# Idle matmuls on zeros in four-wide pieces: 19 of up to 512 columns in place of 73 of 128

## The chip, the core and the metric

The kernel runs on one core of one Trainium2 chip. The metric is the device time of one execution in microseconds; where several executions are given, it is their median. Profiles are of one execution, and their clock starts with the first instruction of the span.

## What is computed

Four batches of eight attention heads (768 tokens, 64 columns to a head) feed a two-layer network. Heads 0, 2 and 6 attend to all earlier tokens; the others attend to the last 64 tokens and to the first four.

```python
scores = scale * q @ k.T                       # each batch and head
keep = causal & (retrieval_head | is_sink | in_window)
a = softmax(where(keep, scores, -1e9))
x = (a @ v).transpose(0, 2, 1, 3).reshape(3072, 512)
h = x @ w_in                                   # 512 -> 2048
g = maximum(h, 0) + alpha * minimum(h, 0)
out = g @ w_out                                # 2048 -> 512
```

## The kernel before

The heads are worked in 16 segments of two heads (four segments to a batch). Of a segment, q, k and v are loaded by SP (`L`), cast to bf16 by VectorE, ScalarE or GpSimd (`C`), transposed (`T`; in the first half of the segments on TensorE, with copies `t` out of PSUM, later by DMA), multiplied to scores (`S`, lines 414, 424 and 431), masked (on TensorE at lines 463 and 502 in batch 0, on VectorE after it), exponentiated by ScalarE (`s`), multiplied with v (`A`, line 553), divided by the row sums (`a`), and transposed into `xT` (`X`). The network runs over eight blocks of tokens: `P` is the first layer (line 598), `p` and `g` its leaky ReLU on ScalarE and VectorE (lines 603 and 610), `O` the second layer (line 618), and `o` the copy out and the store. The very last 128 rows of the output go in three column pieces (`L0` to `L2`, lines 637 and 646).

One list, `ORDER`, written out by hand, says in which order the items are issued; each engine works its own instructions in that order. An engine that comes to an instruction whose data are not there waits, and all behind it on that engine waits too. PSUM has eight banks that the code hands out itself: `take` gives the bank that has been free the longest, `give` returns it.

The change touches the items `warm0` to `warm8`. Each is a run of matmuls on TensorE of a tile of zeros, `busy` (128 x 128, bf16, filled by a VectorE memset at the start), with itself, into a bank that nobody reads before it is written anew. The numbers of matmuls are set here (line 725):

```python
for i, n in enumerate((32, 3, 14, 4, 4, 4, 4, 4, 4)):
    item(f"warm{i}", warm, n)
```

Where they stand on TensorE, by `ORDER`: `warm4`, `warm0` and `warm5` (4 + 32 + 4 = 40 matmuls) are TensorE's first work, ahead of the transposes of the first q and k (`Tq0.0`, `Tk0.0`, line 362). `warm2` (14) follows those transposes, ahead of the first scores (`S0.0.0`, line 414), which need the copies `tq0.0` (ScalarE, line 369) and `tk0.0` (VectorE, line 387). `warm3` and `warm6` (8) stand ahead of twelve transposes (line 364). `warm7` (4) and `warm8` (4) each stand ahead of scores of batch 0 (line 414). `warm1` (3) is TensorE's last work, behind `L1`.

Of the kernel before, what the change touches and what calls it, by code (L numbers as in the profile page):

```python
# [74 lines left out]
def kernel(  # L75
# [13 lines left out]
    nc = tc.nc  # L89
# [54 lines left out]
    def take(*choices):  # L144
        got = min((c for c in choices if all(age[b] >= 0 for b in c)), key=lambda c: max(age[b] for b in c))
        for b in got:
            age[b] = -1
        return got

    def give(got):  # L150
        for b in got:
            age[b] = stamp[0]
            stamp[0] += 1
# [3 lines left out]
    def bank(b):  # L157
        return P[:, b, :]
# [91 lines left out]
    busy = const.tile([128, 128], bf16, name="busy")  # L250
# [432 lines left out]
        nc.vector.memset(eSv[:, i, 5, 192:SLOT].bitcast(fp32), 0.0)  # L683

    def warm(n):
        held["w"] = got = take(*ANY)
        for i in range(n):
            nc.tensor.matmul(bank(got[0])[:, 0:128], busy, busy, start=True, stop=True)  # L688
        give(got)

    def load_w_in(n):
# [33 lines left out]
    for i, n in enumerate((32, 3, 14, 4, 4, 4, 4, 4, 4)):  # L725
        item(f"warm{i}", warm, n)
# [60 lines left out]
    for t in range(8):  # L787
        w = TOK[t][1]
# [59 lines left out]
```

## Time and profile before

| | |
|---|---|
| time, three executions | 228.04, 228.27, 229.32 us; median 228.27 us |
| time of the profiled execution | 228.43 us |
| its span | 225.8 us |
| TensorE matmuls | 221.6 us busy (98%), 2005 instructions |
| TensorE weight loads | 136.5 us (60%), 2005 instructions |
| VectorE, ScalarE, GpSimd | 149.1, 140.1, 45.9 us busy |
| the 73 idle matmuls (line 688) | 7.1 us with TensorE in them |

The 2.6 us between the profiled execution's time and its span lie outside of what the profile shows. PE is the matmul side of TensorE, PEld the loading of its stationary operand, which runs beside the matmuls. A matmul's duration in the profile runs from its start to its modelled end, and the matmuls of a stream overlap; so what a matmul costs in a stream is the distance between two starts, and the duration of a row of x n matmuls is n - 1 such distances and one duration. A row of the timeline reads: start, duration, engine, line, operation, output and input, shapes, how many; in brackets the idle time of the engine ahead of it and what ended that.

### The profile page before, as it was taken

What the parts mean: (1) busy time and instruction counts of PE and PEld (TensorE: products, weight loads), DVE (VectorE), ACT (ScalarE), POOL (GpSimd) and SP (SyncE); (2) the same over time, 40 slices, a digit from 0 to 9 for tenths busy, and PEclk for the clock granted to TensorE, in tenths of its full rate; (3) what the DMA queues carried; (4) which work ended last, traced back from release to release, by engine and by line L of the source; (5) the groups of instructions that cost most, each with busy time, mean ns of one, the idle gap of its engine ahead of it and who ended that gap; (6) DMA issues with size and microseconds to landing.
All of it is one profiled execution on the core that took longest, in us unless ns stands there. A gap on an engine that the chain in (4) does not pass through costs nothing.

```text
span 225.8 us, 5241 instructions
## 1 busy us (share of the span) xinstructions
PE 221.6 (98%) x2005; PEld 136.5 (60%) x2005; DVE 149.1 (66%) x393; ACT 140.1 (62%) x286; POOL 45.9 (20%) x91
## 2 busy tenths in 40 slices
PE   7999999999999999999999999999999999999994
PEld 7989876575556557564556455456556555664454
DVE  5798648986659618897899029977486536866000
ACT  3788669999898036587992147786584237563311
POOL 5679749600230001000400001000110100000000
PEclk9999999999999999999999999999999999999999
DMA  6999999999999999999989999976924420000213
GB/s 201 311 240 214 281 223 285 197 196 231 204 284 182 117 232 231 170 167 190 268 160 177 226 243 129 238 156 117 119 94 38 120 93 0 0 3 1 93 68 119
DMA packets 95417, 37.39 MB, mean 166 GB/s; under 512 B 82440, under 2 KB 93600, under 8 KB 95392
## 3 DMA queue, kind: packets, MB, share of 16 engines
q1 hardware_dynamic: 89136, 27.73, 65.2%
q0 software_dynamic: 5792, 8.93, 17.5%
q10 hardware_dynamic: 464, 0.40, 0.6%
q8 instruction: 15, 0.25, 0.5%
q14 instruction: 10, 0.08, 0.1%
HBM read 27.71 MB, written 6.29 MB: 151 GB/s over the span
## 4 chain that ended last, share of the span: by engine, by line
PE 98%; DVE 0%; issue 0%; DVEq 0%
PE P L598 37%; PE P L618 36%; PE P L553 7%; PE P L431 4%; PE P L414 3%; PE P L688 3%; PE P L364 2%; PE P L637 2%; PE P L424 1%; PE P L502 1%; PE P L578 1%; PE P L463 0%; PE P L362 0%; DVE kT L387 0%; DVE ot L646 0%
## 5 line engine op out<-in xcount | busy, mean ns | idle before, releaser
L610 DVE SCALAR_TENSOR_TENSOR g<-neg,oma,P 128x256 bf16<-128x256 f32 (+1 forms) x128 | 70.9, 608 | 36.9 <-ACT neg L603 36.4
L598 PE MATMUL P<-xT,w_in_b 128*128 128x512 bf16 (+1 forms) x512 | 86.6, 326 | 0.0
L618 PE MATMUL P<-w_out_b,g 128*128 128x512 bf16 x368 | 85.3, 379 | 0.0
L603 ACT ACTIVATE neg<-P 128x512 f32<-128x512 f32 x96 | 54.2, 600 | 26.3 <-PE P L598 20.9
L598 PEld LDWEIGHTS <-w_in_b 128*128 128x128 bf16 x512 | 49.5, 98 | 32.3 <-DVE g L610 0.2
L618 PEld LDWEIGHTS <-g 128*128 128x128 bf16 x368 | 33.9, 98 | 37.2 <-issue 1.0
L470 ACT ACTIVATE eR<-P 128x448 bf16<-128x448 f32 (+4 forms) x63 | 36.9, 635 | 5.8 <-PE P L431 2.5
L624 ACT COPY ot<-P 128x512 f32<-128x512 f32 x23 | 13.9, 605 | 37.1 <-PE P L618 32.3
L628 POOL DMA_DIRECT2D out_dram<-ot x18 | 10.3, 572 | 111.0 <-ACT ot L624 110.8
L518 ACT ACTIVATE eS<-P 128x352 bf16<-128x352 f32 x45 | 20.8, 489 | 3.4 <-PE P L431 3.0
L564 DVE TENSOR_TENSOR xn<-P,rcp 128x448 bf16<-128x448 f32 (+1 forms) x32 | 19.5, 608 | 1.1
L529 DVE TENSOR_TENSOR eS<-eS,ms_near 128x352 bf16<-128x352 bf16 x45 | 14.9, 346 | 0.6 <-ACT eS L518 0.5
L563 DVE RECIPROCAL rcp<-P 128x7 f32<-128x7 f32 (+1 forms) x32 | 6.3, 198 | 10.9 <-PE P L553 10.8
L480 DVE TENSOR_TENSOR eR<-eR,mr_near 128x128 bf16<-128x128 bf16 (+5 forms) x54 | 10.7, 227 | 4.3 <-ACT eR L470 4.1
L414 PE MATMUL P<-qT,kT 128*128 128x192 bf16 (+14 forms) x68 | 11.2, 251 | 0.2 <-DVE kT L387 0.2
L553 PEld LDWEIGHTS <-eS 128*128 128x128 bf16 x260 | 9.5, 97 | 2.3 <-issue 0.6
L553 PE MATMUL P<-vb,eS 128*128 128x65 bf16 x260 | 10.7, 193 | 0.0
L431 PE MATMUL P<-qT,kT 64*128 64x176 bf16 (+10 forms) x168 | 10.5, 252 | 0.0
L431 PEld LDWEIGHTS <-kT 64*128 64x128 bf16 x168 | 6.7, 94 | 6.2 <-issue 5.5
L553 PE MATMUL P<-vb,eR 128*128 128x65 bf16 x276 | 10.5, 193 | 0.0
L553 PEld LDWEIGHTS <-eR 128*128 128x128 bf16 x276 | 9.5, 97 | 1.3
L646 DVE COPY ot<-P 128x128 f32<-128x128 f32 x1 | 0.3, 291 | 14.3 <-PE P L637 14.3
(95 smaller groups left out, 177.3 us busy)
## 6 DMA issues: line engine op xcount, KB each, us to landing
out_dram<-ot POOLq DMA_DIRECT2D x18, 256.0 KB, 3.9
kf<-in_k_dram SPq DMA_DIRECT2D x21, 192.0 KB
qf<-in_q_dram SPq DMA_DIRECT2D x18, 192.0 KB
vf<-in_v_dram SPq DMA_DIRECT2D x14, 196.0 KB
qf<-in_q_dram SPq DMA_DIRECT2D x7, 384.0 KB
vf<-in_v_dram SPq DMA_DIRECT2D x12, 192.0 KB
w_in_b<-in_moe_w_in_dram POOLq DMA_DIRECT2D x8, 256.0 KB, 9.6
w_out_b<-in_moe_w_out_dram POOLq DMA_DIRECT2D x4, 512.0 KB, 13.9
```

The source lines that it names most:

```text
L414: nc.tensor.matmul(to, keys, queries, start=True, stop=stop)
L431: nc.tensor.matmul(to, keys[own], queries[own], start=True, stop=True)
L470: nc.scalar.activation(ebuf[n, hh][:, lo:hi].rearrange("p (x c) -> p x c", x=len(parts)), P[:, got[0]:got[0] + len(parts), 0:(hi - lo) // ...
L518: nc.scalar.activation(slots, sc[:, 0:352].rearrange("p (s c) -> p s c", c=176), AF.Exp, scale=scale)
L529: nc.vector.tensor_tensor(slots, slots, ms_near[:, 0:2, :] if m == 0 else ms_near[:, 1:3, :], op=ALU.mult)
L553: nc.tensor.matmul(pav[:, i, :], e[:, o:o + 128], vv[:, j, hh, 0:D + 1], start=(m == 0), stop=(m == len(terms) - 1))
L564: nc.vector.tensor_tensor(xn[n][:, 0:nt, D * hh:D * hh + D], pav[:, :, 0:D], rcp.to_broadcast([128, nt, D]), op=ALU.mult)
L598: nc.tensor.matmul(psg[:, w * i:w * (i + 1)], w_in_b[:, c, 128 * fb:128 * (fb + 1)], xT[:, c, o:o + w], start=(x == 0), stop=(x == 3))
L603: nc.scalar.activation(neg[t, f], bank(held["P", t, f][0]), AF.Relu, scale=-1.0)
L610: nc.vector.scalar_tensor_tensor(g_buf[t % 2][:, fb, 0:w], neg[t, f][:, c], oma[:, fb:fb + 1], bank(got[0])[:, c], op0=ALU.mult, op1=ALU.add)
L618: nc.tensor.matmul(bank(held["O", t, s][0]), g_buf[t % 2][:, f, 128 * s:128 * (s + 1)], w_out_b[:, f, :], start=(f == 0), stop=(f == 15))
L624: nc.scalar.copy(ot, bank(got[0]))
```

## The change

`warm(n)` issues its matmuls in pieces of up to four. The stationary operand is still `busy`. The moving operand is `busy` read w times in a row, through an access pattern with a step of zero, and the output is 128 * w columns of the bank. So 32, 14, 4 and 3 matmuls of 128 columns become 8 of 512; 3 of 512 and one of 256; one of 512; and one of 384: 19 in place of 73, with 9344 columns in both. A weight load goes with each matmul, so there are 19 in place of 73 of these too. All else, `ORDER` included, is as it was: the order and the waits of all other instructions are the same on every engine.

```diff
     def warm(n):
+
         held["w"] = got = take(*ANY)
-        for i in range(n):
-            nc.tensor.matmul(bank(got[0])[:, 0:128], busy, busy, start=True, stop=True)
+        for i in range(0, n, 4):
+            w = min(4, n - i)
+            nc.tensor.matmul(bank(got[0])[:, 0:128 * w].rearrange("p (a c) -> p a c", c=128), busy,
+                             busy.unsqueeze(1).to_broadcast([128, w, 128]), start=True, stop=True)
         give(got)
```

## The prediction

> **What bounds the kernel now.** I read the page's chain of waits first, to see on whose work the end hangs, and then only the stretches in which line 688, the idle matmuls, runs.
>
> ```profile
> span 225.8 us, 5241 instructions
> PE 221.6 (98%) x2005; PEld 136.5 (60%) x2005; DVE 149.1 (66%) x393; ACT 140.1 (62%) x286; POOL 45.9 (20%) x91
> ...
> PE 98%; DVE 0%; issue 0%; DVEq 0%
> ```
>
> The chain that ended last is TensorE's for 98% of the span. What is saved or lost there counts in full, unless TensorE then stands waiting for something else. So the questions are whether the same columns take the same time in wider pieces, and what ends the waits behind each idle stretch.
>
> The instructions of line 688:
>
> ```profile
> L688 PEld LDWEIGHTS <-busy x73: 96/150/152, 1.2 to 222.6; 128*128 128x128 bf16 x73
> L688 PE MATMUL P<-busy x73: 219/314/315, 1.2 to 222.7; 128*128 128x128 bf16 x73
> ```
>
> The median matmul takes 314 ns and the shortest 219: the same instruction at two speeds. The timeline shows where each holds, and what the work behind the idle matmuls needs:
>
> ```profile
> 1.20 4.18 PEld L688 LDWEIGHTS <-busy 128*128 128x128 bf16 x40 [1.20 <-DVE busy L288]
> 1.21 4.45 PE L688 MATMUL P<-busy 128*128 128x128 bf16 x40 [1.21 <-DVE busy L288]
> ...
> 4.47 0.30 DVE L319 CAST g<-qf 128x384 bf16<-128x384 f32 x1
> ...
> 4.89 0.51 ACT L328 CAST g<-kf 128x384 bf16<-128x384 f32 x1 [1.88 <-DMA kf<-in_k_dram]
> ...
> 5.58 0.90 PE L362 MATMUL P<-ident,g 128*64 128x128 bf16 x12
> 6.19 0.79 ACT L369 COPY qT<-P 64x768 bf16<-64x768 bf16 x1 [0.78 <-PE P L362]
> ...
> 6.42 0.96 PE L688 MATMUL P<-busy 128*128 128x128 bf16 x14
> 6.52 1.01 DVE L387 COPY kT<-P 64x258 bf16<-64x258 bf16 x2 [1.76 <-PE P L362]
> ...
> 7.21 0.35 PE L414 MATMUL P<-qT,kT 128*128 128x448 bf16 x1
> ...
> 8.47 0.61 PE L688 MATMUL P<-busy 128*128 128x128 bf16 x8
> ...
> 219.09 1.03 PE L618 MATMUL P<-w_out_b,g 128*128 128x512 bf16 x4
> ```
>
> The first 40 start (4.45 - 0.314) / 39 = 0.106 us apart. The eight at 8.47 start (0.61 - 0.219) / 7 = 0.056 us apart. TensorE runs at half rate to begin with. By the start times in the trace the distance falls from 0.107 to 0.056 us between the second and the third transpose of line 362, and the trace's record of the granted clock has its first entry, at the full share, at 5.72 us. (The page's PEclk digits read 9 ahead of that too, since time without an entry is counted as full there.) So the gate opened 5.72 - 1.21 = 4.51 us after the first idle matmul.
>
> **The first stretch, 40 narrow matmuls into 10 wide ones.** Before: 40 x 0.106 = 4.26 us. A wide one at half rate is not in this trace. At full rate it is: the four of line 618 start (1.03 - 0.379) / 3 = 0.217 us apart, against 4 x 0.056 = 0.224 us for the same columns in narrow ones. So a matmul costs its columns and almost nothing besides, and at half rate I take 4 x 0.106 = 0.425 us: 10 x 0.425 = 4.25 us. No change, to 0.01 us. The weight loads, 40 before and 10 after, run beside the matmuls in both.
>
> The lower bound is the full rate at once, 10 x 0.217 = 2.17 us, so 2.1 us less on TensorE. The path doesn't get that. The second six transposes need the k cast, done by ScalarE at 4.89 + 0.51 = 5.40 us, and by the trace the seventh of the twelve starts at 5.99. So whatever the idle matmuls save here, the path gains 0.59 us at most, and then waits for k. The upper bound is a moving operand with a step of zero that is read at half speed, for which no row of this trace exists: 4.25 us more. The nearest row is line 618, another 128x512 bf16 operand, and I take its price.
>
> **The stretches at full rate.** `warm2`, 14 x 0.056 = 0.78 us, becomes 3.5 x 0.217 = 0.76. `warm3` and `warm6`, 0.45 us, become 0.43. `warm7` and `warm8`, 0.22 us each, lose 0.007 each. Together some 0.05 us less on TensorE. Little of it reaches the end. The first scores need the q copy of ScalarE, done at 6.19 + 0.79 = 6.98, and start at 7.21, so that 0.02 us can move ahead. But at 12.5 us TensorE waits for VectorE:
>
> ```profile
> 12.20 1.03 DVE L387 COPY kT<-P 64x258 bf16<-64x258 bf16 x2
> ...
> 12.69 0.36 PE L414 MATMUL P<-qT,kT 128*128 128x448 bf16 x1 [0.17 <-DVE kT L387]
> ```
>
> VectorE is without a gap from 8.04 us to there, beginning with a memset of kT that no idle matmul decides. What TensorE saved ahead of 12.69 is spent in that wait. `warm8` alone lies behind it: 0.01 us on the path.
>
> At the one place where a page differs from the rows, the Trainium skill ("TensorE: Matmul & The Clock Gate", section "Back-to-back issue gap") gives the sustained distance with a weight load to each matmul as about 81 ns at 128 columns and 131 ns at 512. By that, the full-rate stretches alone would go from 30 x 81 = 2.4 us to some 7.5 x 131 = 1.0 us, an estimate of 1.4 us less. The rows here, 56 and 217 ns, disagree at both widths.
>
> **The end.** `warm1`, three into one, is TensorE's last work.
>
> ```profile
> 222.59 0.33 PE L688 MATMUL P<-busy 128*128 128x128 bf16 x3
> 222.85 0.29 DVE L646 COPY ot<-P 128x128 f32<-128x128 f32 x1 [14.32 <-PE P L637]
> 223.16 0.33 SPq L647 DMA_DIRECT2D out_dram<-ot  x1
> ```
>
> The end hangs on the copy at 222.85 and its store at 223.16; the idle matmuls stand behind the last real one and end at 222.92, covered by the copy, which runs to 223.14. Nothing waits for them. One of 384 columns (between 0.22 and 0.38 us by the rows of 128 and 512 columns) is covered too; it would show only if it ran beyond the 2 us of store behind it.
>
> **What else moves.** Nothing: no DMA is issued at another place of a queue, and no bank or wait of the other instructions changes. TensorE's instruction stream is 108 shorter; from 30 us to the end of its last matmul at 222.92 the windows show TensorE without idle time (192.92 us busy), so no shorter wait for instructions is there to gain.
>
> **Sum.** 0.00 (first stretch) - 0.01 (full rate) + 0.00 (end) = -0.01 us against the profiled execution's 228.43: 228.42. That execution is 0.16 us above the median of the three runs, which would go to 228.26. The gate's opening also differs between executions: each us that it comes later costs half a us, since only half the columns pass until then, and the three times, 228.04 to 229.32, are spread by 1.28 us as 2.6 us of difference in its opening would make them. So I put the median at 228.3, with 227.6 to 229.4 for the forecast's own range. Less than 0.5%, 1.14 us, is about what a measurement of this kernel can't tell from no change.
>
> **Rival 1, slower: the gate opens late.** If what opens it counts weight loads as well as matmuls, the first stretch changes. Before, PEld was busy for 4.18 of its 4.45 us; after, ten loads of 0.15 us make 1.5 us. If that falls short, the count starts again with the transposes at 5.58 us, which have a load to each 128 columns, and the gate opens 4.51 us behind them, at 10.09. Work between 5.72 and 10.09 then passes at half rate: 4.37 / 2 = 2.19 us more, 230.5. The point from which it decides is whether the gate opens inside the stretch up to about 7.5 us or not. For it: the loads are the only activity that the change takes away. Against it: matmul streaming is as dense as before, and wide matmuls with one load each hold the full clock through lines 598 and 618. Chance 0.24. By the Trainium skill (same page, section "What's actually happening") the gate is set by windows of 3413 ns that run freely, so that it would open one window late, at 9.13 us: an estimate of 1.7 us more. The same passage counts time and not matmuls, which speaks against this rival; no run shown here has wide matmuls at a cold start.
>
> **Rival 2, slower: the zero step is slow.** At half speed the first stretch costs 4.25 us more, `warm2` and the others 1.6 us more, less what waits hide: some 234. Against it: each column is read from the same places as before, and at 128 columns that ran at full rate; the trace has nothing nearer. Chance 0.03.
>
> **Rival 3, faster: the gate opens early, or wide matmuls beat it.** The first stretch is capped at 0.59 us by the k cast: 227.7, which is inside 0.5%. To pass 1.14 us, the later work would have to give as much again, and the wait at 12.69 us takes what is saved ahead of it. Favourable phases of the gate in few runs could do the rest: some 227.0. Chance 0.09.
>
> **How the numbers follow.** The forecast, no change to 0.5%, has 0.64, including gains up to the cap; slower has 0.24 + 0.03 = 0.27; faster 0.09. The forecast's own range leaves out too much, so the range goes up to rival 1's 230.5, and down to 227.4, below the cap's 227.7 by the spread of the gate; outside are rival 2, the later half of rival 1, and most of rival 3.
>
> **What would show it.** Right: ten wide matmuls 0.42 to 0.43 us apart from 1.2 to about 5.45 us, the first transposes at 5.5 to 5.6, the wide ones behind them 0.217 apart, first scores at about 7.2, the wait for VectorE at 12.7, and a last store at about 223.2. Rival 1: transposes of line 362 and scores of line 414 at half rate, a first entry of the clock record behind 8 us. Rival 2: distances of 0.85 us in the first stretch. The forecast is wrong if the first scores move by over 1 us with that still seen behind 20 us.

## The result, and the profile after

| | before | wide pieces |
|---|---|---|
| median of 22 executions each | 228.09 us | 229.42 us |
| lowest, highest | 226.88, 231.74 us | 227.96, 231.33 us |
| profiled execution: time, span | 228.43, 225.8 us | 230.24, 228.5 us |

The wide pieces are slower: the ratio is 1.0056, with an interval of 1.0031 to 1.0082, and the medians are 1.3 us apart. That is just over what I called no change (0.5%), and inside the range, 227.4 to 230.5. The place from which it comes is not one that the prediction names. An execution more than 1.5% above the fastest of its kernel, such as the 231.74 us before, is left out of the ratios here and below.

The page of the profiled execution, which is one of the slower half (230.24 us):

```profile
span 228.5 us, 5133 instructions
...
PE 221.7 (97%) x1951; PEld 132.6 (58%) x1951; DVE 149.2 (65%) x393; ACT 140.2 (61%) x286; POOL 45.9 (20%) x91
...
PE 83%; DMA 9%; POOL 2%; SPq 2%; issue 1%; ACT 1%; ACTq 0%; DVE 0%; POOLq 0%; DVEq 0%
PE P L618 35%; PE P L598 34%; DMA kf<-in_k_dram 7%; PE P L553 6%; PE P L431 4%; DMA qf<-in_q_dram 3%; PE P L637 2%; PE P L424 1%; SPq L223 1%; PE P L364 1%; POOL g L315 1%; POOL w_in_b L696 1%; ACT eR L470 0%; SPq L246 0%; POOL g L328 0%
```

TensorE's busy time is as before, 221.7 against 221.6 us, and the span is 2.7 us longer. The chain was TensorE's for 98%; now 9% of it is loads, of k and q. In what follows, the gate opens where TensorE passes from half to full rate; the trace's clock record begins there. The head of the timeline (the idle matmuls are line 690 here) came out as forecast:

```profile
1.21 4.18 PE L690 MATMUL P<-busy 128*128 128x512 bf16 x10 [1.21 <-DVE busy L288]
...
5.05 0.51 ACT L328 CAST g<-kf 128x384 bf16<-128x384 f32 x1 [2.04 <-DMA kf<-in_k_dram]
...
5.32 0.86 PE L362 MATMUL P<-ident,g 128*64 128x128 bf16 x12
5.87 0.79 ACT L369 COPY qT<-P 64x768 bf16<-64x768 bf16 x1 [0.31 <-PE P L362]
...
6.11 0.93 PE L690 MATMUL P<-busy 128*128 128x512 bf16 x4
...
6.87 0.35 PE L414 MATMUL P<-qT,kT 128*128 128x448 bf16 x1
```

By the start times the wide matmuls are 0.427 us apart at half rate and 0.216 behind it. The gate opened at 4.98 us, 3.77 us behind the first idle matmul (4.51 before), and the first scores start 0.34 us earlier than before. So at 7 us this execution was ahead. Who waited for whom on TensorE, before:

```profile
PE P L688 <- DVE busy L288: 1.2, 1, 1.2
PE P L414 <- DVE kT L387: 0.2, 1, 0.2
```

and after:

```profile
PE P L364 <- POOL natm L328: 1.9, 1, 1.9
PE P L690 <- DVE busy L288: 1.2, 1, 1.2
PE P L364 <- POOL g L315: 0.5, 1, 0.5
PE P L553 <- POOL vb L306: 0.2, 1, 0.2
PE P L414 <- DVE kT L387: 0.2, 1, 0.2
```

Columns: who waited for whom, us in all, times, longest. The waits for casts are 1.9 + 0.5 + 0.2 = 2.6 us; before there were none. The longest one in the timeline of GpSimd and TensorE, before:

```profile
31.93 0.51 POOL L328 CAST natm<-kf 128x384 bf16<-128x384 f32 x1 [1.91 <-DMA kf<-in_k_dram]
```

```profile
34.28 0.50 PE L364 MATMUL P<-ident,natm 128*128 128x128 bf16 x6
```

and after:

```profile
33.70 0.50 POOL L328 CAST natm<-kf 128x384 bf16<-128x384 f32 x1 [2.94 <-DMA kf<-in_k_dram]
36.40 0.51 POOL L328 CAST natm<-kf 128x384 bf16<-128x384 f32 x1 [2.20 <-DMA kf<-in_k_dram]
```

```profile
36.96 0.51 PE L364 MATMUL P<-ident,natm 128*128 128x128 bf16 x6 [1.93 <-POOL natm L328]
```

After, GpSimd waits for k from DRAM, and TensorE for GpSimd; before, the transposes waited for nothing. The load of k came 4.5 us later than before, though the change touches no load. What is different far ahead of it is GpSimd's work at 12 to 16 us. Before:

```profile
13.19 0.83 POOL L315 CAST g<-qf 128x768 bf16<-128x768 f32 x1 [1.20 <-DMA qf<-in_q_dram]
...
15.64 1.41 POOL L693 DMA_DIRECT2D w_in_b<-in_moe_w_in_dram  x2
17.04 0.85 POOL L315 CAST g<-qf 128x768 bf16<-128x768 f32 x1
```

and after:

```profile
12.18 0.83 POOL L315 CAST g<-qf 128x768 bf16<-128x768 f32 x1
...
14.63 1.41 POOL L696 DMA_DIRECT2D w_in_b<-in_moe_w_in_dram  x2
18.35 0.83 POOL L315 CAST g<-qf 128x768 bf16<-128x768 f32 x1 [2.31 <-DMA qf<-in_q_dram]
```

After, q of the third segment is there without a wait, 1 us earlier; so the loads of w_in, which stand behind it in GpSimd's queue, are issued 1 us earlier; and the next load of q ends at least 1.3 us later. One thing that the change does move in the DMA traffic is TensorE's own instructions. They are fetched in blocks of 16 KB over a DMA queue of their own (q8 in the page; its packets take 0.9 to 2.0 us each in these two traces). That q8 is TensorE's follows from a count: from the first fetch to the sixth TensorE starts 1301 matmuls and weight loads before and 1253 after, 250 to 260 to a block. With 108 instructions fewer, all but four of them ahead of 16 us, TensorE comes to each block later: by the trace's records of q8 the first three fetches stand at 9.81, 20.39 and 27.15 us before, at 14.51, 23.38 and 30.68 after. The Trainium skill ("Runtime: NRT & Kernel Launch", section "Instruction fetch mechanics") describes these 16 KiB blocks of 256 instructions and the sequencer's own DMA queue, and calls their cost mostly hidden. For TensorE the trace agrees: the list of its waits above has none for instructions of its own.

### The profile page after: what moved, and what is told of

Read it like the earlier page. It is cut to its first block, busy times and chain, and to the rows that moved or that the text cites. A ratio compares the mean times of both kernels' runs of the same rounds, so it can differ in the third digit from the quotient of the medians.

```text
span 228.5 us, 5133 instructions
## 1 busy us (share of the span) xinstructions
PE 221.7 (97%) x1951; PEld 132.6 (58%) x1951; DVE 149.2 (65%) x393; ACT 140.2 (61%) x286; POOL 45.9 (20%) x91
## 4 chain that ended last, share of the span: by engine, by line
PE 83%; DMA 9%; POOL 2%; SPq 2%; issue 1%; ACT 1%; ACTq 0%; DVE 0%; POOLq 0%; DVEq 0%
PE P L618 35%; PE P L598 34%; DMA kf<-in_k_dram 7%; PE P L553 6%; PE P L431 4%; DMA qf<-in_q_dram 3%; PE P L637 2%; PE P L424 1%; SPq L223 1%; PE P L364 1%; POOL g L315 1%; POOL w_in_b L696 1%; ACT eR L470 0%; SPq L246 0%; POOL g L328 0%
## 5 line engine op out<-in xcount | busy, mean ns | idle before, releaser
L529 DVE TENSOR_TENSOR eS<-eS,ms_near 128x352 bf16<-128x352 bf16 x45 | 14.3, 333 | 0.6 <-ACT eS L518 0.5
```

Source lines behind the costliest of these rows:

```text
L529: nc.vector.tensor_tensor(slots, slots, ms_near[:, 0:2, :] if m == 0 else ms_near[:, 1:3, :], op=ALU.mult)
```

## The experiments

The theories: **S**, the length of TensorE's instruction stream decides, through the time of its fetches; **G**, the gate opens later behind wide matmuls (the prediction's first rival); **R**, the wide pieces at full rate do it; **L**, half of S, that the time is lost in waits for late k and q. Each kernel was timed in 12 executions (`narrow_64` in 6) beside the kernel before on the same chip, and each ratio is to that.

**One part of the change at a time.** `e1_first_wide`: the wide form for the first three items, the narrow one for the others.

```diff
+        begun.append(n)
...
+        if len(begun) <= 3:
+            for i in range(0, n, 4):
...
+        else:
+            for i in range(n):
+                nc.tensor.matmul(bank(got[0])[:, 0:128], busy, busy, start=True, stop=True)
```

> Only the first 40 idle matmuls become 10 wide ones; the 33 later ones stay narrow. Theory S (the stream: TensorE has 60 instructions fewer at its head here, 108 fewer in the changed kernel, so its blocks of instructions are fetched at other times against the loads, and a load of k comes late): slower than before, by half to all of the changed kernel's 1.3 us, with a wait of TensorE for a k or q cast between 18 and 36 us. Theory G (the gate opens later behind wide matmuls): all of the 1.3 us, with the first entry of the clock record behind 6 us in most executions. Theory R (the wide ones behind the first stretch, at full rate, do it): no change, within 0.3 us.

Measured: ratio 1.0041 (1.0006 to 1.0075). `e2_rest_wide` is the same with `> 3`:

> Only the 33 idle matmuls behind the first stretch become 9 wide ones; the first 40 stay narrow. Theory S: 48 instructions fewer, all of them ahead of 16 us but three pairs: slower by up to 1.3 us, less surely than with the first stretch wide. Theory G: no change, within 0.3 us, since nothing ahead of the gate's opening changes. Theory R: all of the 1.3 us.

Measured: 1.0006 (0.9983 to 1.0028). By the ratios the first stretch carries the loss, against R, though the two intervals overlap. In e1's profile (228.16 us) the gate opened at 4.56 us, earlier than before, and TensorE waits for casts (0.3 us each for k and q, 0.2 for v): against G, as far as one execution goes. In e2's profile (229.26 us) it waits for casts too, 0.8 us for k and 0.4 for v, though the ratio shows no change.

**The old length of the stream, with empty instructions.** `e3_first_wide_nops` is e1 with this behind each wide matmul, and `e7_wide_nops60` is the changed kernel with it behind the first ten:

```diff
+                for x in range(2 * (w - 1)):
+                    nc.tensor.nop(nofuse=True, hint="idle")
```

> The first 40 idle matmuls become 10 wide ones, with six empty instructions on TensorE's queue behind each, so that TensorE's stream has as many instructions as before and each later one has its old place. Theory S: as before, within 0.3 us. Theory G: slower by 1.3 us, like the kernel with the first stretch wide alone. Theory R: no change, within 0.3 us. If an empty instruction costs more than 0.04 us the first stretch grows, which its profile would show as distances over 0.43 us.

> The changed kernel with six empty instructions behind each of its first ten wide matmuls, so that the instructions behind the first stretch stand where they would with 40 narrow ones; the later stretches stay wide. Theory S (the loads land later because TensorE's blocks of instructions are fetched later): within 0.3 us of before, as with the later stretches wide alone, and the first fetch at 11 us or earlier. Theory G, and any cause in the matmuls themselves: 1.0 to 1.3 us above before. The second fetch's place is still some 48 instructions off.

Measured: e3 1.0019 (0.9995 to 1.0043), e7 1.0015 (0.9989 to 1.0041). Both lie between the two forecasts, near that of S. The empty instructions start 0.07 us apart in the trace, so six of them take as long as a wide matmul, and the first stretch grew: the transposes began at 5.82 us in e7. e7's first fetch stood at 12.16 us, not at 11 or earlier. So these two lean to S and don't settle it.

`e4_narrow_64` leaves the matmuls narrow and puts two such instructions behind each of `warm0`'s:

> All idle matmuls stay narrow; 64 empty instructions go between the first ones, two behind each of 32. Theory S: the blocks of instructions are fetched earlier by a quarter of a block; the time moves, by up to 1 us either way, while no matmul differs. Theories G and R: no change, within 0.3 us, if the first stretch keeps its 4.3 us.

Measured: 1.0088 (1.0062 to 1.0113). The condition of the expectation failed: the first stretch grew by 1.4 us (transposes at 7.02 us) and the gate opened at 9.47 us. It tells nothing of S. It does show what a longer first stretch and a late gate look like: 2 us more without one wait for a cast.

**Is it the loads?** `e5_light_narrow` and `e6_light_wide` are the two kernels with a quarter of w_in loaded (the matmuls of line 598, not shown in this cut, then read the same 128 columns for four blocks):

```diff
-                            dram(moe_w_in, 4 * D * hh * d_ff + lo, [[d_ff, D], [D * d_ff, 4], [1, 512]]))
+                            dram(moe_w_in, 4 * D * hh * d_ff + lo, [[d_ff, D], [D * d_ff, 4], [1, 128]]))
```

> The kernel before, but each load of w_in brings 128 columns in place of 512, and every four first-layer blocks use the same weights (this part of the computation is changed); TensorE's work is the same, the loads ahead of 36 us are lighter by three quarters of w_in. By itself: TensorE waits for no k or q cast, and the time is at most that of before, 227 to 228 us. It is there to be compared with the next kernel.

> The changed kernel with the same lighter loads of w_in. Theory L (the changed kernel's extra time is TensorE waiting for k and q that land later): within 0.3 us of the light narrow kernel, and no wait for a cast between 18 and 36 us. Theory G (the gate opens later behind wide matmuls): 1.0 to 1.3 us above the light narrow kernel, with a later first entry of the clock record.

Measured against the kernel before: narrow 1.0007 (0.9986 to 1.0028), wide 1.0000 (0.9981 to 1.0020). The whole difference is gone. The waits of TensorE in the light wide kernel:

```profile
PE P L690 <- DVE busy L288: 1.2, 1, 1.2
PE P L414 <- DVE kT L387: 0.2, 1, 0.2
```

None is for a cast, and the last k cast begins at 29.10 us, where the changed kernel had 36.40. The 12 times lie between 227.50 and 228.47 us. This kernel has the same wide first stretch as the changed one, so what the gate's opening varied in these 12 is within that 1 us; the changed kernel's times of 230 to 231 aren't explained by it. L holds, G falls.

**The changed kernel once more.**

> The changed kernel once more, beside the other three on the same chip: 1.3 us above before. Its profile is a second sample. Theory L: a wait of TensorE for a cast of k or q between 18 and 36 us, of 0.5 us or more in all. Theory G: no such wait, and a first entry of the clock record behind 7 us.

Measured: 1.0043 (1.0011 to 1.0076). Here both expectations on the profile missed: the profiled execution was the fastest of the 12, 227.50 us, and has no wait for a cast, against L, and its gate opened at 4.95 us, against G. The times show why one profile can't be enough: 227.50, then five between 228.08 and 228.30, then six from 230.03 up. The loss is not one of every execution. That k comes too late in the slower ones is read from one profile, the first one of the changed kernel, at 230.24 us.

**The old length without the longer stretch.** In `e9_wide_filled` the 108 missing instructions are half further weight loads of the zeros, half empty instructions, three of each beside a wide matmul:

```diff
+            for x in range(w - 1):
+                nc.tensor.ldweights(busy)
+                nc.tensor.nop(nofuse=True, hint="idle")
```

`e10_wide_loads` has the weight loads alone, and `e11_first_filled` has both, with the first stretch wide only.

> The changed kernel, all pieces wide, with a further weight load of the same zeros and an empty instruction for each matmul that a wide one replaced: 54 and 54, so that TensorE's stream is as long as before at every point, and weight loads are as many as before. (Six empty instructions, 0.07 us each, lengthened the first stretch by 0.3 us; three fit beside a matmul of 0.43 us.) Theory S (the length of the stream decides, through the times at which its blocks are fetched): within 0.3 us of before, first fetch at 9.5 to 11.5 us, few runs above 229 us. Against it, if width itself costs: 1.0 to 1.3 us above before, with runs above 230 us.

> The changed kernel with the 54 further weight loads alone: as many weight loads as before, half of the missing instructions restored. Theory S: between, 0.2 to 1.0 us above before, first fetch between 11.5 and 13.5 us. The prediction's rival that the gate counts weight loads: as before, and the gate open in the first stretch only here and not in the changed kernel, against what the changed kernel's profile shows.

> Only the first 40 idle matmuls in 10 wide pieces, with 30 further weight loads and 30 empty instructions among them; the later ones narrow. The stream has its old length everywhere. Theory S: within 0.3 us of before. If width itself costs: 1.0 us above, like the first stretch wide without these.

Measured: e9 0.9973 (0.9946 to 1.0001), e10 1.0020 (0.9992 to 1.0048), e11 0.9977 (0.9953 to 1.0001). All as S has it, e9 with all pieces wide. A rival is an earlier gate in these kernels (3.99 us in e9, 4.88 in e11). In e11 it falls: its first scores start at 6.84 us, the changed kernel's at 6.87, so the two heads keep the same time, and none of e11's 12 times is above 229.16. GpSimd's work in e9 is back where it was before, to 0.05 us:

```profile
13.15 0.83 POOL L315 CAST g<-qf 128x768 bf16<-128x768 f32 x1 [1.14 <-DMA qf<-in_q_dram]
...
15.60 1.41 POOL L699 DMA_DIRECT2D w_in_b<-in_moe_w_in_dram  x2
17.02 0.83 POOL L315 CAST g<-qf 128x768 bf16<-128x768 f32 x1
```

To that precision it is chance: in the profile of e12, the same kernel once more, these rows stand 0.5 us later.

Since e9 seemed a little faster than both kernels, it was run again:

> The wide pieces with 54 further weight loads and 54 empty instructions once more, since its first time was 0.3% below before with an interval that just reached no change. Theory S alone: the same as before, within 0.2%. If the wide pieces with the old length of the stream are a gain of their own: 0.2 to 0.3% below before again, and 0.8% below the changed kernel.

Measured: 1.0014 (0.9990 to 1.0037). It isn't faster; e9 and e12, the same kernel, lie around no change. No version here beats the kernel before by more than the noise.

**All together**, by the instructions missing from TensorE's stream. The four times (us) are of the one profiled execution; the last of them is how long GpSimd waits for the next q, behind the issue of w_in. e3 is left out: its profiled execution took 234.39 us, with the second layer's matmuls 0.224 us apart in place of 0.216.

| kernel | missing | first fetch | w_in issued | last k cast | wait for q | ratio |
|---|---|---|---|---|---|---|
| before | 0 | 9.81 | 15.64 | 31.93 | none | 1 |
| e9 wide, filled | 0 | 9.78 | 15.60 | 31.77 | none | 0.9973 |
| e12 the same | 0 | 11.29 | 16.16 | 33.11 | none | 1.0014 |
| e11 first wide, filled | 0 | 9.52 | 15.38 | 33.14 | 0.18 | 0.9977 |
| e2 rest wide | 48 | 11.32 | 15.54 | 34.62 | 0.19 | 1.0006 |
| e7 wide, 60 empty | 48 | 12.16 | 14.68 | 35.50 | 1.59 | 1.0015 |
| e10 wide, loads | 54 | 12.15 | 14.71 | 32.65 | 1.46 | 1.0020 |
| e1 first wide | 60 | 12.26 | 15.99 | 33.72 | 0.48 | 1.0041 |
| e8 wide again | 108 | 13.92 | 14.77 | 33.19 | 1.44 | 1.0043 |
| wide pieces | 108 | 14.51 | 14.63 | 36.40 | 2.31 | 1.0056 |

Among the kernels with wide pieces the time goes with the missing instructions by and large; no kernel with narrow matmuls and a shorter stream was run. The last k cast of a single profile doesn't go with the ratio. The single times show it more plainly: of those that enter the ratios, 10 of the changed kernel's 31 are above 230 us, 3 of e1's 10, 1 of the 34 of e2, e7 and e10, 1 of the 43 of e3, e9, e11 and e12, and none of the 125 of the kernel before.

**What stays open.** Shown are both ends: the length of the stream decides, and the time is lost in loads of k and q that lighter loads of w_in make harmless. Between them the fetches are what the runs leave as the link, but no run moved a fetch by itself. One sign of them stands in all fourteen profiles: where the first fetch comes at 11.32 us or earlier (eight of them), GpSimd waits 0.34 us or less for the next q, and where it comes at 12.15 us or later (six), 0.48 to 2.31 us. That parts e2 from e7, which miss equally many instructions. In e6 the fetch comes at 14.06 us and the wait is 1.41 us, so lighter loads of w_in don't remove this wait, but they do remove the later ones for k. The path from a fetch at 14 instead of 10 us to a k that is late at 32 (the earlier issue of w_in, or the fetch beside the loads of v) is argued and not shown; in the table, e1 has w_in issued late and is slow all the same.

## Why the prediction was right or wrong

- **The first stretch** was right: 0.427 us per wide matmul at half rate where 0.425 was taken, and no price for the step of zero or the smaller number of weight loads. The transposes started at 5.32 us, and not between 5.5 and 5.6, since the gate opened at 4.98 us in this execution and the last wide matmul ran at full rate.
- **The full-rate stretches** were right: 0.216 us at 512 columns, and e2 at no change. The 81 and 131 ns of the Trainium skill ("TensorE: Matmul & The Clock Gate", section "Back-to-back issue gap") are at neither width what the trace shows, 56 and 216 ns.
- **The wait at 12.69 us** was misread. It was to take up what TensorE saves ahead of it, because VectorE works without a gap from 8.04 us. But that run of VectorE's hangs on the first transposes too (its copy at 6.52 us waits for them), and it moved with them:

```profile
6.21 1.01 DVE L387 COPY kT<-P 64x258 bf16<-64x258 bf16 x2 [1.44 <-PE P L362]
...
11.89 1.03 DVE L387 COPY kT<-P 64x258 bf16<-64x258 bf16 x2
...
12.37 0.36 PE L414 MATMUL P<-qT,kT 128*128 128x448 bf16 x1 [0.17 <-DVE kT L387]
```

After the change the first scores start 0.34 us earlier, and those behind the wait 0.32; the wait is as long as before. The saving passes through, and the forecast didn't suffer because there was next to nothing to save.
- **The end** was right: line 690's last matmul, 0.33 us, is covered by the copy behind it, 0.29 us from 225.53.
- **The step that failed is "What else moves. Nothing".** It asked only whether TensorE waits for its instructions, and it never did. The fetch of those instructions is itself traffic, and it moved by 3 to 5 us against loads that keep the DMA engines at 90% and more there, by the page's second part. It had no term in the sum; by the difference of the measured medians it is worth 1.3 us. That the fetch is what carries it is, as said, the likeliest link and not shown alone.
- **Rival 1** had the right sign and the wrong cause. Its price, 2.2 us from a late gate, is near the 1.7 us between the two groups of times in e8, but the gate opened within 3.8 us behind the first idle matmul in both profiles of the changed kernel, and with the weight loads put back (e10) it opened later, about 6.0 us behind it by the distances of the matmuls, not earlier. That the measured median lies inside the range is in part luck: the upper end stood there for this rival.
- **The spread of the times** was put down to the gate. In e6, where no cast is waited for, the times spread over 1 us (in e5 over 2.1), the changed kernel's over 3.4; so much of its spread goes with the loads.
- **Rival 3's cap** shows in e12, where the gate opened at 3.88 us: the first transposes start at 4.82 us, but the seventh only at 5.48, behind the k cast that ends at 5.42. As a gain in time it wasn't tested.

## What to carry to other kernels

A kernel whose loads keep the DMA engines busy may depend on all that uses those engines, and in this one the program's own instructions seem to count: taking instructions out of TensorE's head changed when all its later blocks were fetched. A wait takes up a saving only if the other side of it doesn't move with the saving, so follow that side back too. To find out whether an edit acts through what it computes or through its length, put the length back with instructions that cost nothing beside the work, and look whether the time comes back. And where single executions differ by 2 us, read a profile together with its own time: it may show the half in which nothing went wrong.

## What was not expected of the hardware

- The gate opened 2.67 us (e12) and 2.78 us (e9) behind the first idle matmul, 4.51 before, and about 5.3 in e6 (by the distances of the transposes). The Trainium skill ("TensorE: Matmul & The Clock Gate", section "What's actually happening") has it open after a busy window of some 3.4 us that runs freely. The trace agrees with the free running: this spread, and open stretches of 218.45, 221.87 or 225.28 us in all ten clock records, 64, 65 and 66 times 3.413. But 2.67 us is not a whole window of work.
- In e4 the narrow matmuls were 0.16 us apart, not 0.107, once the empty instructions slowed them, and the gate opened only 8.3 us behind the first.
- Empty instructions on TensorE's queue start 0.07 us apart. Beside wide matmuls at half rate three to a matmul, with three weight loads, are free (0.427 us apart in e9); six are not (0.445 to 0.485 us in e7).
